# Two PSUM pools instead of one, feed-forward work in smaller parts, and the key and query products moved from GpSimd to VectorE

## The chip, the cores and the metric

The kernel runs on one core of a Trainium2 chip. The core has a matrix engine (TensorE, PE in the profile, with its weight loads as PEld), a vector engine (VectorE, DVE), an activation engine (ScalarE, ACT), a general engine (GpSimd, POOL) and a queue for transfers (SyncE, SP). Matrix products land in PSUM, which this kernel uses as eight banks of 512 fp32 numbers for each of 128 partitions. The metric is device time in microseconds for the whole program; the inputs lie in device memory before it and the output lies there after it.

## The reference, cut to what matters

Two blocks follow each other. The first is a recurrent attention with a complex gate, for 4 batches, 8 heads, 768 positions and 48 features a head; the second is a feed-forward block with a maximum over three products.

```python
def _attn_ref(q, k, v, a_re, a_im):
    mag = np.sqrt(a_re * a_re + a_im * a_im)
    scale = np.minimum(mag, 0.999) / (mag + 1e-06)
    a_re_n, a_im_n = (a_re * scale, a_im * scale)
    for t in range(S):                      # S = 768
        new_re = ar * S_re - ai * S_im      # S_re, S_im: (B, H, D, D)
        new_im = ar * S_im + ai * S_re
        S_re, S_im = (new_re + k[t] v[t], new_im)
        y[t] = q[t] S_re

def _moe_ref(x, w1, w2, w3, w_out):         # x: 3072 x 384, w1..w3: 384 x 768
    h = np.maximum(np.maximum(x @ w1, x @ w2), x @ w3)
    return h @ w_out                        # 3072 x 384
```

The kernel does not step through positions one by one. It takes 128 positions of one batch as a tile (24 tiles, two to a group, so 12 groups), turns the gate into a logarithm of its size (`Ln`) and an angle, sums these within the tile by matrix products, scales the keys and queries by the exponentials of the sums, and gets the scores, the carried state and the output from matrix products. Everything is fp32.

## The kernel before: the parts that the change touches

Every PSUM tile comes from one pool with one tag: four rooms of two banks each, which go round in the order in which the tiles are asked for.

```python
    psum = ctx.enter_context(tc.tile_pool(name="psum", bufs=4, space=PSUM))
    # ...
    def banks(nm, n=None):
        ps = psum.tile([P, 2, 512], FP, tag="ps", name=nm)
        return ps if n is None else ps.rearrange("p a n -> p (a n)")[:, 0:n]
```

From group 2 on, the matrix engine's order is fixed as written (`chained`): each matrix product is tied behind the last. The orders of the other engines come from the scheduler when the program is built.

The products of keys and queries with their decays stand behind the sums. `E` has two buffers.

```python
    def products(x):
        g, c = divmod(x, C)
        def s0():
            ps = banks("sums")
            # ... 8 matrix products
            En = T["En", x] = nat2.tile([P, DM], FP, tag="En", name="En")
            act(out=En.rearrange("p (c n) -> p c n", c=2), in_=ps[:, :, HC:2 * HC], func=AF.Exp, scale=-1.0)
            for nm, sg in (("k", 1.0), ("q", -1.0)):
                E = nat2.tile([P, DM], FP, tag="E", name="E")
                act(out=E.rearrange("p (c n) -> p c n", c=2), in_=ps[:, :, 0:HC], func=AF.Exp, scale=sg)
                eng = nc.gpsimd if g > 1 else nc.vector
                eng.tensor_tensor(out=hd(T[nm, x]), in0=E, in1=hd(T[nm, x]), op=OP.mult)
        # ...
```

The scores come in two tiles. `A` is put into the score matrix `atm` by four masked copies on VectorE; after them ScalarE copies `B` into the same `atm`.

```python
    def scores(x, nm):
        ps = banks(nm)
        # ... "A": 32 matrix products of 80 columns, "B": 16 of 32 columns
    def gather(x, nm):
        atm = T["atm", x] = atms[x % 2]
        if nm == "A":
            # ... nc.vector.copy_predicated, four times, from T["A", x]
        else:
            src = T[nm, x][:, 0, 0:H * 32].rearrange("p (h t) -> p h t", h=H)
            for o in (0, L64):
                nc.scalar.copy(out=atm[o:o + 32, :, 32:], in_=src[o:o + 32])
```

The feed-forward block: a step takes three column blocks of 128 (`n = 3`), so its PSUM tile is 768 numbers wide for the two tiles of a group. The first of three weights is copied to `hT` by ScalarE, the second and third are joined by a maximum on VectorE.

```python
    def up_step(xs, fs, i):
        # ...
        ps = banks("up", len(fs) * n).rearrange("p (f t) -> p f t", t=n)
        for j, f in enumerate(fs):
            for d in range(KD):
                mm(out=ps[:, j], lhsT=ws[i][:, d, f * P:(f + 1) * P], rhs=xT[:, d],
                                 start=(d == 0), stop=(d == KD - 1))
        if i == 0:
            nc.scalar.copy(out=dst, in_=ps)
        else:
            nc.vector.tensor_tensor(out=dst, in0=dst, in1=ps, op=OP.max)

    def out_step(xs, x):
        ps = banks("op", DM)
        for f in range(KF):
            mm(out=ps, lhsT=hT[:, f, o:o + P], rhs=wo[:, f], start=(f == 0), stop=(f == KF - 1))
        ot = fp2.tile([P, DM], FP, tag="ot", name="ot")
        nc.scalar.copy(out=ot, in_=ps)
        # ... store

    def ffn_steps(xs):
        n = 2 if xs[0] == 0 else 3
        return [call(up_step, xs, range(f, f + n), i) for f in range(0, KF, n) for i in range(3)] \
            + [call(out_step, xs, x) for x in xs]
```

One group mixes attention for its tiles x and y with the feed-forward steps of the group before and the gates of the groups after. `feed(n)` issues the next n feed-forward steps; `pairs` is both scores with their gathers; `turned` holds the transposes (`tp`, evicted to `K` and `Q`), the cut sums (`F`, evicted to `f` by four ScalarE exponentials), and the state (`dk`, added to `g` by VectorE); `sums` are the two `s0` above; `turning` holds the angles (`cs`); `later` are the gates of the group after next.

```python
        if g > 1:
            feed(1)
        pairs(x)
        if g > 1:
            gates[2]()
        feed(1)
        # ...
        turned(y)
        sums[0]()
        sums[1]()
        feed(1)
        outputs(x, tokens(x))
        rest(y)
        turning()          # feeds 2 steps before its matrix products
        pairs(y)
        units[0]()
        units[1]()
        for f in later:
            f()
        feed(2)
        turned(y + 1)
        feed(1)
        outputs(y, tokens(y))
        rest(y + 1)
        feed(len(ffn))
```

Of the kernel before, what the change touches and what calls it, by code (L numbers as in the profile page):

```python
# [51 lines left out]
def kernel(  # L52
# [22 lines left out]
    C = 2  # L75
# [484 lines left out]
    def scores(x, nm):  # L560

        ps = banks(nm)
        for h in range(H):
            if nm == "A":
                for o in range(0, P, 32):
                    mm(out=ps[o:o + 32, h // HU, h % HU * P:h % HU * P + 80], lhsT=T["K", x][0:DD, h, o:o + 32],
                       rhs=T["Q", x][0:DD, 4 * h + o // 32], start=True, stop=True)
            else:
                for j in range(2):
                    o = j * L64  # L570
                    mm(out=ps[o:o + 32, 0, h * 32:h * 32 + 32], lhsT=T["KB", x][0:DD, 2 * h + j],
                       rhs=T["QB", x][0:DD, 2 * h + j], start=True, stop=True)
        T[nm, x] = ps

    def gather(x, nm):
# [24 lines left out]
        else:  # L600
            src = T[nm, x][:, 0, 0:H * 32].rearrange("p (h t) -> p h t", h=H)
            for o in (0, L64):
# [58 lines left out]
    def up_step(xs, fs, i):  # L661
        xT, n = T["xT", xs[-1]], len(xs) * P
        if fs[0] == 0 and i == 0:

            T["hT", xs[-1]] = ld2.tile([P, KF, n], FP, tag="ar", name="hT") if xs[0] == 0 else \
                fp2.tile([P, KF, n], FP, tag="hT", padded_shape=[P, KF, TG], name="hT")
        dst = T["hT", xs[-1]][:, fs[0]:fs[-1] + 1]
        ps = banks("up", len(fs) * n).rearrange("p (f t) -> p f t", t=n)
        for j, f in enumerate(fs):
            for d in range(KD):  # L670
                mm(out=ps[:, j], lhsT=ws[i][:, d, f * P:(f + 1) * P], rhs=xT[:, d],
                                 start=(d == 0), stop=(d == KD - 1))
        if i == 0:
            nc.scalar.copy(out=dst, in_=ps)  # L674
        else:
            nc.vector.tensor_tensor(out=dst, in0=dst, in1=ps, op=OP.max)  # L676

    def out_step(xs, x):
        hT, o = T["hT", xs[-1]], (x - xs[0]) * P
        ps = banks("op", DM)  # L680
        for f in range(KF):
            mm(out=ps, lhsT=hT[:, f, o:o + P], rhs=wo[:, f], start=(f == 0), stop=(f == KF - 1))
        ot = fp2.tile([P, DM], FP, tag="ot", name="ot")
        nc.scalar.copy(out=ot, in_=ps)
        t0 = x // C // NS * C * S + x % C * S + x // C % NS * P
        nc.sync.dma_start(out=out[t0:t0 + P, :], in_=ot)

# [85 lines left out]
    weave((0.0, 1.0, tile_steps(0) + tile_steps(1)), (0.0, 0.7, rounds), (0.15, 0.58, pre_steps(1)),  # L773
          (0.415, 0.44, ffn[:6]), (0.55, 0.75, ffn[6:9]), (0.25, 0.27, [call(load, 1, load_v)]), (0.6, 0.62, [call(load, 2, load_a)]),
          (0.75, 1.0, gate_steps(2, list(range(C)))))
# [4 lines left out]

    held = ffn[9:]

    def group(g):
        x, y = g * C, g * C + 1
        load(g + 1, load_v)
        if g > 1:
            load(g + 2, load_a, load_kq)
        ffn = held + ffn_steps(tokens(x - 1))
        held[:] = [ffn.pop()]

        def feed(n):
            for _ in range(min(n, len(ffn))):
                ffn.pop(0)()
# [36 lines left out]
        sums[1]()  # L830
        feed(1)
        outputs(x, tokens(x))
# [14 lines left out]
    for g in range(1, NG):  # L847
        if g == 2:
            T["chain"] = None
        group(g)  # L850
    for f in held + ffn_steps(tokens(NX - 1)):
        f()
# [30 lines left out]
```

## Time and profile before

| what | value |
|---|---|
| time, median of 3 runs | 667.38 us (666.75 to 668.34) |
| span of the profiled execution | 666.7 us |
| PE busy | 581.8 us (87%), 10076 instructions |
| PEld busy | 472.5 us (71%) |
| DVE busy | 476.9 us (72%), 638 instructions |
| ACT busy | 404.2 us (61%), 670 instructions |
| POOL busy | 122.4 us (18%), 131 instructions |
| chain that ended last, by engine | PE 46%, ACT 24%, DVE 16% |
| granted PE clock, mean | 0.963 |

The busy time of an engine is the union of its instructions' times. "Idle before, releaser" in the profile is the time an engine stood still before an instruction, and what ended it. The chain that ended last is followed back from the last instruction, at each step to what released it. The first 150 us or so are a ramp, in which the weights are loaded and brought into shape; after it the kernel repeats one pattern for each group, and that pattern is what the windows of the trace show best.

### The profile page before, as it was taken

Reading aid. Unit: us, or ns where it says so; the run is one execution under the profiler, and the core shown is the slowest. Engines: PE = TensorE matmul, PEld = TensorE weight load, DVE = VectorE, ACT = ScalarE, POOL = GpSimd, SP = SyncE. Lnnn points to the kernel's source line nnn. Section 1 sums busy time; section 2 is a strip of 40 time slices with the busy share of each in tenths; the row PEclk is TensorE's granted clock in tenths of the full one; section 3 lists DMA queues with packets and bytes.
Section 4 is the critical chain, followed back from the end, with each engine's and each line's share of the span. In section 5 each row is a group of like instructions: output and inputs, shape, how many; then the busy total and the mean of one; then the engine's idle time right before and its main releaser. Section 6 shows DMA issues by size and latency. Waiting matters only on the chain.

```text
span 666.7 us, 22815 instructions
## 1 busy us (share of the span) xinstructions
PE 581.8 (87%) x10076; PEld 472.5 (71%) x10076; DVE 476.9 (72%) x638; ACT 404.2 (61%) x670; POOL 122.4 (18%) x131
## 2 busy tenths in 40 slices
PE   1244777898999999999999999999999999999997
PEld 0143665777877878868868867878878777878785
DVE  3899998985777877877776687778778777655111
ACT  6889696577476567567566665765764854631000
POOL 9400102305113114013014013023023023000000
PEclk9956898997999999999999999999999999999999
DMA  6975542330330330330330420421320210000000
GB/s 134 272 166 142 139 83 56 62 62 14 61 65 24 61 69 19 65 69 15 73 61 15 83 52 24 76 53 35 67 56 15 40 47 3 2 27 2 19 7 24
DMA packets 136547, 39.26 MB, mean 59 GB/s; under 512 B 129152, under 2 KB 132224, under 8 KB 136448
## 3 DMA queue, kind: packets, MB, share of 16 engines
q1 hardware_dynamic: 136448, 37.80, 26.1%
q8 instruction: 79, 1.29, 0.8%
q14 instruction: 20, 0.16, 0.1%
HBM read 33.03 MB, written 4.72 MB: 57 GB/s over the span
## 4 chain that ended last, share of the span: by engine, by line
PE 46%; ACT 24%; DVE 16%; issue 8%; DMA 3%; SPq 2%; POOL 1%; DVEq 0%; POOLq 0%; ACTq 0%
PE up L117 24%; PE op L117 12%; DVE Q L533 6%; PE y L117 3%; ACT CS L112 3%; ACT f L112 2%; ACT L133 2%; ACT e L112 2%; PE A L117 2%; ACT Q L505 2%; PE cs L117 2%; ACT K L501 2%; PE dk L117 2%; DVE g L632 2%; DMA ai<-in_a_im_dram 1%
## 5 line engine op out<-in xcount | busy, mean ns | idle before, releaser
L117 PE MATMUL up<-xT,w 128*128 128x256 f32 (+1 forms) x1404 | 295.9, 369 | 11.0 <-ACT f L112 4.5
L117 PEld LDWEIGHTS up<-xT,w 128*128 128x128 f32 x1404 | 249.0, 192 | 46.9 <-ACT f L112 7.7
L533 DVE TENSOR_TENSOR Q<-Q,f 112x512 f32<-112x512 f32 (+2 forms) x72 | 91.6, 1278 | 49.2 <-ACT f L112 49.2
L117 PE MATMUL op<-wo,hT 128*128 128x384 f32 x288 | 99.0, 494 | 0.5 <-ACT K L501 0.4
L117 PEld LDWEIGHTS op<-wo,hT 128*128 128x128 f32 x288 | 53.2, 190 | 34.9 <-DVE hT L676 0.8
L674 ACT COPY hT<-up 128x768 f32<-128x768 f32 (+2 forms) x27 | 19.6, 727 | 91.8 <-PE up L117 91.7
L676 DVE TENSOR_TENSOR hT<-hT,up 128x768 f32<-128x768 f32 (+2 forms) x54 | 46.4, 859 | 38.8 <-PE up L117 38.7
L381 POOL TENSOR_TENSOR ai<-ai,L 128x768 f32<-128x768 f32 x10 | 22.3, 2226 | 276.9 <-ACT L L112 188.0
L117 PE MATMUL A<-Q,K 112*32 112x80 f32 x1536 | 34.7, 247 | 12.8 <-DVE Q L533 12.8
L117 PEld LDWEIGHTS A<-Q,K 112*32 112x32 f32 x1536 | 29.9, 117 | 21.8 <-issue 13.6
L117 PE MATMUL y<-atm,vb 128*32 128x64 f32 x1152 | 39.5, 224 | 0.9 <-issue 0.7
L117 PEld LDWEIGHTS y<-atm,vb 128*32 128x32 f32 x1152 | 32.6, 112 | 10.4 <-issue 5.6
L112 ACT ACTIVATE f<-F 48x280 f32<-48x280 f32 x96 | 38.3, 399 | 0.9
L117 PE MATMUL y<-QG,g 112*32 112x64 f32 x1408 | 38.3, 220 | 0.0
L487 DVE TENSOR_TENSOR uk<-uk,En 128x768 f32<-128x768 f32 x24 | 24.5, 1021 | 18.0 <-PE tp L117 18.0
L477 POOL TENSOR_TENSOR k<-E,k 128x384 f32<-128x384 f32 x20 | 25.6, 1279 | 63.7 <-ACT E L112 63.7
L389 POOL TENSOR_TENSOR ai<-ai,carry 1x768 f32<-1x768 f32 x10 | 18.6, 1864 | 92.8 <-ACT ai L386 92.8
L117 PE MATMUL sums<-Ln,mid 64*64 64x192 f32 x192 | 15.8, 378 | 22.7 <-DVE Ln L371 22.7
L117 PEld LDWEIGHTS y<-QG,g 112*32 112x32 f32 x1408 | 34.9, 110 | 0.4 <-ACT g L630 0.2
L477 POOL TENSOR_TENSOR q<-E,q 128x384 f32<-128x384 f32 x20 | 34.9, 1747 | 0.0
L117 PE MATMUL cs<-w,upto 128*64 128x192 f32 x192 | 20.1, 355 | 15.7 <-DVE w L400 15.7
L412 DVE SCALAR_TENSOR_TENSOR nf<-t,cs 128x384 f32<-128x384 f32 x24 | 13.3, 554 | 28.5 <-ACT t L410 27.4
(103 smaller groups left out, 949.9 us busy)
## 6 DMA issues: line engine op xcount, KB each, us to landing
ar<-in_a_re_dram SPq DMA_DIRECT2D x24, 192.0 KB
ai<-in_a_im_dram SPq DMA_DIRECT2D x24, 192.0 KB
k<-in_k_dram SPq DMA_DIRECT2D x96, 48.0 KB
q<-in_q_dram SPq DMA_DIRECT2D x96, 48.0 KB
vb<-in_v_dram SPq DMA_DIRECT2D x96, 48.0 KB
out_dram<-ot SPq DMA_DIRECT2D x24, 192.0 KB
raw<-in_moe_w_dram SPq DMA_DIRECT2D x5, 768.0 KB
w<-in_moe_w_dram SPq DMA_DIRECT2D x2, 768.0 KB
```

The source lines that it names most:

```text
L112: tab(nc.scalar.activation(**kw))
L117: ins = f(**kw)
L133: tab(nc.scalar.preload_act_table_set(nm))
L381: (nc.gpsimd if g > 1 else nc.vector).tensor_tensor(out=ai, in0=ai, in1=L, op=OP.mult)
L389: nc.gpsimd.tensor_tensor(out=ai[0:1], in0=ai[0:1], in1=T["carry", g], op=OP.subtract)
L477: eng.tensor_tensor(out=hd(T[nm, x]), in0=E, in1=hd(T[nm, x]), op=OP.mult)
L487: nc.vector.tensor_tensor(out=u, in0=u, in1=two(T["En", x]), op=OP.mult)
L501: nc.scalar.copy(out=T["K", x][0:DD].rearrange("p n (j t) -> p j n t", j=2), in_=src)
L505: nc.scalar.copy(out=T["Q", x][0:DD, :, 0:32].rearrange("p (n j a) t -> p j n a t", n=H, j=2), in_=src.rearrange("p j n (a t) -> p j n a t ...
L533: nc.vector.tensor_tensor(out=out, in0=in_, in1=f.to_broadcast([DD, 2 * H - g, n, 8]), op=OP.mult)
L674: nc.scalar.copy(out=dst, in_=ps)
L676: nc.vector.tensor_tensor(out=dst, in0=dst, in1=ps, op=OP.max)
```

## The change

The PSUM pool is split in two: `psum2` with three rooms of two banks, for the tiles that need two (`A`, `tp`, `F`, `dk`, `sums`), and `psum1` with two rooms of one bank, for the others (`B`, `cs`, `y`, `up`, `op`). The eight banks are as before all in use, as five rooms and not four. So that a feed-forward tile fits one bank, a step takes two column blocks in place of three, in all tiles. The steps are cut into parts (half an `up` step, a third of an `op` step) which `feed` counts, and `feed` is called at one more place, between the transposes and the state, so that the matrix engine has work there. Last, the products of keys and queries are made by VectorE for all groups; before, GpSimd made them for the groups 2 to 11. What is computed stays the same.

```diff
-    psum = ctx.enter_context(tc.tile_pool(name="psum", bufs=4, space=PSUM))
+    psum1 = ctx.enter_context(tc.tile_pool(name="psum1", bufs=2, space=PSUM))
+    psum2 = ctx.enter_context(tc.tile_pool(name="psum2", bufs=3, space=PSUM))
@@ banks
-        ps = psum.tile([P, 2, 512], FP, tag="ps", name=nm)
-        return ps if n is None else ps.rearrange("p a n -> p (a n)")[:, 0:n]
+        if n is None:
+            return psum2.tile([P, 2, 512], FP, tag="two", name=nm)
+        return psum1.tile([P, 512], FP, tag="one", name=nm)[:, 0:n]
@@ products
-                eng = nc.gpsimd if g > 1 else nc.vector
+                eng = nc.vector
@@ scores
-        ps = banks(nm)
+        ps = banks(nm, None if nm == "A" else H * 32)
@@ up_step, now a list of parts (out_step alike, three parts of two blocks each)
+        def part(j, f):
+            # ...
+            if j == 0:
+                box["ps"] = banks("up", len(fs) * n).rearrange("p (f t) -> p f t", t=n)
             for d in range(KD):
-                mm(out=ps[:, j], lhsT=ws[i][:, d, f * P:(f + 1) * P], rhs=xT[:, d],
+                mm(out=box["ps"][:, j], lhsT=ws[i][:, d, f * P:(f + 1) * P], rhs=xT[:, d],
+            # ... the eviction after the last part
+        return [call(part, j, f) for j, f in enumerate(fs)]
@@ ffn_steps
-        n = 2 if xs[0] == 0 else 3
-        return [call(up_step, xs, range(f, f + n), i) for f in range(0, KF, n) for i in range(3)] \
-            + [call(out_step, xs, x) for x in xs]
+        return [up_step(xs, (f, f + 1), i) for f in range(0, KF, 2) for i in range(3)] \
+            + [out_step(xs, x) for x in xs]
@@ group
-        ffn = held + ffn_steps(tokens(x - 1))
-        held[:] = [ffn.pop()]
+        ffn = held + every_part(ffn_steps(tokens(x - 1)))
+        held[:] = ffn[-3:]
+        del ffn[-3:]
-        pre = pre_steps(g + 1, feed) if g + 1 < NG else [lambda: None] * 8
+        pre = pre_steps(g + 1, lambda n: feed(2 * n)) if g + 1 < NG else [lambda: None] * 8
@@ turned
                 cut(x)
+            feed(2)
             state(x - 1)
@@ the body of the group
         if g > 1:
-            feed(1)
+            feed(3)
         pairs(x)
         ...
-        feed(1)
+        feed(2)
         ...
         sums[1]()
-        feed(1)
+        feed(2)
         outputs(x, tokens(x))
         ...
-        feed(2)
+        feed(6)
         turned(y + 1)
-        feed(1)
+        feed(3)
         outputs(y, tokens(y))
```

More of the change, by code (lines that the diff above doesn't have):

```diff
@@ L570, in scores @@
                     o = j * L64
-                    mm(out=ps[o:o + 32, 0, h * 32:h * 32 + 32], lhsT=T["KB", x][0:DD, 2 * h + j],
+                    mm(out=ps[o:o + 32, h * 32:h * 32 + 32], lhsT=T["KB", x][0:DD, 2 * h + j],
                        rhs=T["QB", x][0:DD, 2 * h + j], start=True, stop=True)
@@ L600, in gather @@
         else:
-            src = T[nm, x][:, 0, 0:H * 32].rearrange("p (h t) -> p h t", h=H)
+            src = T[nm, x].rearrange("p (h t) -> p h t", h=H)
             for o in (0, L64):
@@ L661, in up_step @@
     def up_step(xs, fs, i):
[L662 to L669, printed above, removed]
-            for d in range(KD):
-                mm(out=ps[:, j], lhsT=ws[i][:, d, f * P:(f + 1) * P], rhs=xT[:, d],
-                                 start=(d == 0), stop=(d == KD - 1))
@@ L673, in up_step @@
[L673 to L676, printed above, removed]
-    def out_step(xs, x):
[L679 to L686, printed above, removed]
+        n, box = len(xs) * P, {}
@@ new lines, in part @@
+        def part(j, f):
+            xT = T["xT", xs[-1]]
+            if f == 0 and i == 0:
+                T["hT", xs[-1]] = ld2.tile([P, KF, n], FP, tag="ar", name="hT") if xs[0] == 0 else \
+                    fp2.tile([P, KF, n], FP, tag="hT", padded_shape=[P, KF, TG], name="hT")
+            if j == 0:
+                box["ps"] = banks("up", len(fs) * n).rearrange("p (f t) -> p f t", t=n)
+            for d in range(KD):
+                mm(out=box["ps"][:, j], lhsT=ws[i][:, d, f * P:(f + 1) * P], rhs=xT[:, d],
+                   start=(d == 0), stop=(d == KD - 1))
+            if j < len(fs) - 1:
+                return
+            dst = T["hT", xs[-1]][:, fs[0]:fs[-1] + 1]
+            if i == 0:
+                nc.scalar.copy(out=dst, in_=box["ps"])
+            else:
+                nc.vector.tensor_tensor(out=dst, in0=dst, in1=box["ps"], op=OP.max)
@@ new lines, in up_step, with part @@
+        return [call(part, j, f) for j, f in enumerate(fs)]
+    def out_step(xs, x):
+        box = {}
+        def part(j):
+            hT, o = T["hT", xs[-1]], (x - xs[0]) * P
+            if j == 0:
+                box["ps"] = banks("op", DM)
+            for f in (2 * j, 2 * j + 1):
+                mm(out=box["ps"], lhsT=hT[:, f, o:o + P], rhs=wo[:, f], start=(f == 0), stop=(f == KF - 1))
+            if j < KF // 2 - 1:
+                return
+            ot = fp2.tile([P, DM], FP, tag="ot", name="ot")
+            nc.scalar.copy(out=ot, in_=box["ps"])
+            t0 = x // C // NS * C * S + x % C * S + x // C % NS * P
+            nc.sync.dma_start(out=out[t0:t0 + P, :], in_=ot)
+        return [call(part, j) for j in range(KF // 2)]
@@ L703, in ffn_steps, with every_part @@
     def ffn_steps(xs):
-        n = 2 if xs[0] == 0 else 3
-        return [call(up_step, xs, range(f, f + n), i) for f in range(0, KF, n) for i in range(3)] \
-            + [call(out_step, xs, x) for x in xs]
+        return [up_step(xs, (f, f + 1), i) for f in range(0, KF, 2) for i in range(3)] \
+            + [out_step(xs, x) for x in xs]
+    def every_part(steps):
+        return [part for step in steps for part in step]
     def front(x):
@@ L773 @@
     weave((0.0, 1.0, tile_steps(0) + tile_steps(1)), (0.0, 0.7, rounds), (0.15, 0.58, pre_steps(1)),
-          (0.415, 0.44, ffn[:6]), (0.55, 0.75, ffn[6:9]), (0.25, 0.27, [call(load, 1, load_v)]), (0.6, 0.62, [call(load, 2, load_a)]),
+          (0.415, 0.44, every_part(ffn[:6])), (0.55, 0.75, every_part(ffn[6:9])), (0.25, 0.27, [call(load, 1, load_v)]), (0.6, 0.62, [call(load, 2, load_a)]),
           (0.75, 1.0, gate_steps(2, list(range(C)))))
     load(2, load_kq)
-    held = ffn[9:]
+    held = every_part(ffn[9:])
     def group(g):
@@ L850 @@
         group(g)
-    for f in held + ffn_steps(tokens(NX - 1)):
+    for f in held + every_part(ffn_steps(tokens(NX - 1))):
         f()
```

## The prediction

> **What bounds it now.** I read the busy times by window first, to see what limits the repeating part; then the waits in that part; then the order of instructions in one group. The windows' columns are: busy time and count of PE, PEld, DVE, ACT and POOL, the granted PE clock, and the DMA share.
>
> ```profile
> 50.00:100.00 50.00, 30.61 (x642) 26.88 (x638) 47.43 (x72) 42.70 (x69) 1.81 (x1) 0.81 0.52 121
> 250.00:300.00 50.00, 48.27 (x883) 38.70 (x885) 38.54 (x49) 31.82 (x53) 9.89 (x6) 1.00 0.26 51
> ```
>
> In the ramp VectorE is full (47.43 of 50) and TensorE waits. From about 200 us on TensorE is busy for 48.27 of 50 us at full clock and VectorE has a quarter of its time free. A group lasts 48.95 us there: its first `A` starts at 250.62, the next group's at 299.56. So TensorE bounds eight or nine of the twelve groups, and each microsecond that it stands still is lost. What stops it, in one group:
>
> ```profile
> 260.67 4.15 PE L117 MATMUL up<-xT,w 128*128 128x256 f32 x18 [0.44 <-ACT f L112]
> 267.15 8.04 PE L117 MATMUL up<-xT,w 128*128 128x256 f32 x36 [0.60 <-DVE g L633]
> 288.56 1.14 PE L117 MATMUL dk<-vb,uk 64*64 64x48 f32 x64 [0.68 <-DVE hT L676]
> ```
>
> Each of the three waits for a PSUM room, of `F`, `dk` and `up`. They make 0.44 + 0.60 + 0.68 = 1.72 us a group, so the group's own matrix work is 48.95 - 1.72 = 47.2 us. That is all that better rooms can win: 1.7 us in each of some nine groups, 15 us.
>
> **The Trainium skill.** Three places bear on it. "GPSIMD Engine Reference", 3.1 Elementwise, puts a two-input elementwise operation on GpSimd at 1.96 times VectorE's time. The trace has a larger ratio: 1.32 (k) and 1.72 us (q) median on GpSimd, 0.57 us for the same 128x384 shape on VectorE in the first groups. Section 1, Specifications, says GpSimd shares its SBUF interfaces with VectorE, with contention when VectorE has two SBUF inputs. The trace agrees: the state's first product, a 112x384 with two SBUF inputs, takes 1.35 us at 263.60, while GpSimd makes q, and 0.55 us at 293.45, while it does nothing. "TensorE: Matmul & The Clock Gate" says two things: in "Architectural detail", that ScalarE and VectorE are strictly first in, first out; in Part 1, that the clock halves after an idle window of some 3.4 us. The trace agrees with the second after a stop of 4.70 us:
>
> ```profile
> 102.36 2.36 PE L117 MATMUL A<-Q,K 112*32 112x80 f32 x64 [4.70 <-DVE Q L533]
> 276.57 1.31 PE L117 MATMUL A<-Q,K 112*32 112x80 f32 x64
> ```
>
> The same 64 instructions took 2.36 us after the stop and 1.31 us without.
>
> **Part by part: the products.** Forty of them, four for each of ten groups, leave GpSimd: 20 x 1.279 + 20 x 1.747 = 60.5 us off an engine that nobody in the repeating part waits for long. On VectorE they cost 40 x 0.57 = 22.8 us, 2.3 us a group. VectorE gets about as much back, since the products that ran beside GpSimd (Q 1.95 for 1.22, g 1.35 for 0.55) shrink by some 2 us. In busy time this part is nearly neutral; in order it is not, as the four stand in VectorE's queue ahead of `hT`.
>
> **Part by part: smaller steps.** Evictions of `up` go from 27 to 39 on ScalarE and 54 to 78 on VectorE, with the same elements in all. A 128x768 takes 0.95 us on VectorE and a 128x256 0.41, so about 0.14 us fixed each: 24 x 0.14 = 3.4 us on VectorE, 12 x 0.16 = 2 us on ScalarE. Beside TensorE this hides.
>
> **Part by part: the rooms.** Here the path changes. The order in which the changed program is built fixes who waits for whom. The one-bank tiles now have two rooms, so each waits until the tile two places earlier is evicted; before, it was four places. I walk through a group with the durations above. An `up` step is now 6 products, which the trace records as 12 instructions; 36 of them took 7.97 us, so a step is 12 x 0.221 = 2.66 us. A takes 1.2 us, B 0.6, the two transposes and F 1.7, dk 1.1, sums 1.85, y 1.7, cs 1.45, an `op` step 4.07.
>
> First half, A at 0: the `up` steps, transposes, dk and sums find their rooms free, because the masked copies end at about 3.4 and B's copy at 4.1. The third `up` ends at 14.25 and y at 15.95. The next `up` needs the room of the third, whose maximum is behind this line on VectorE, from F's exponentials at 8.6: Q (0.61), Q (1.14), hT (0.55), Q (0.87), g, KB, g, QB, g (0.46 or 0.60 each), four products (0.45 to 0.57, the third and fourth held by E's two buffers), hT. That is done at about 17.2. TensorE waits 1.2 us. cs then starts at about 22.6.
>
> Second half, cs at 0: A, B and one `up` follow and end at 5.85. The second `up` takes the room of B. Before, B's room was wanted only after two steps of 4 us and a transpose. ScalarE frees it with its copy into `atm`, and this copy now stands in ScalarE's order behind the angles' functions, a table load, and three of the gates' functions (L, w, e). The kernel before shows how long those take:
>
> ```profile
> 276.03 0.49 ACT L410 ACTIVATE t<-cs 128x384 f32<-128x384 f32 x1
> ...
> 280.58 1.28 ACT L133 ACT_TABLE_LOAD   x1
> 281.88 0.84 ACT L112 ACTIVATE L<-L 128x768 f32<-128x768 f32 x1
> 282.63 0.72 ACT L603 COPY atm<-B 32x256 f32<-32x256 f32 x2
> 283.37 0.84 ACT L112 ACTIVATE w<-L 128x768 f32<-128x768 f32 x1
> 284.12 0.83 ACT L112 ACTIVATE e<-L 128x768 f32<-128x768 f32 x1
> ```
>
> From the first t (0.85 after cs starts) to the end of the table load is 281.86 - 276.03 = 5.83, so 6.7; L, w and e add 0.75 + 0.75 + 0.85, B's copy 0.72: done at 9.75. TensorE waits 9.75 - 5.85 = 3.9 us, in each group from 2 to 9. In group 10, without gates after it, the copy follows the table load and the wait is 1.5.
>
> A third stop: the second `op` needs the room of the first, whose copy on ScalarE stands behind the next gate's square, which waits for w on VectorE, behind the whole chain Q to g. By the same sums that square is done at about 28.4 after cs, the copy at 28.9, and TensorE wants the room at 26.8 (all with the 3.9 us stop). 1 to 2 us more; I take 1.6.
>
> **The sum.** Stops of 1.2 + 3.9 + 1.6 = 6.7 us in place of 1.72: +5.0 us a group. A stop of 3.9 us may halve the clock; a window of 3.4 us falls mostly into it about half the time, and costs some 1.7 us then: +0.9. Eight groups: 8 x 5.9 = 47. Group 10 about +1, the tail 0 (only `up` and `op` steps, VectorE free). In the ramp VectorE is full, and takes up 4 x 0.57 for group 2 and the more evictions: +3. Together +51, so 718 us.
>
> **Rivals.** First, the rooms do what they are for: the three waits of 1.72 us go, VectorE and GpSimd no longer meet, and the time falls by up to 15 us to 652. For it: all three waits are for rooms, and there are five rooms now. Against it: the two rooms of the short tiles are wanted sooner than they are freed, by the order as built; one B in each group is enough. Second, VectorE becomes the bound by its load: 477 + 23 + 3 - 20 = 483 us of some 670 says no; in a group it has 38.5 of 49 us. It would give 670 to 680. Third, the stops are there, but shorter, since the engines run ahead of my walk: only the 3.9 us one, and at full clock: 8 x (3.9 - 1.7) = 18, so 685. Against it: all three stops follow from ScalarE's and VectorE's own orders.
>
> **Range and chances.** The stop behind B is the surest: it is one chain of ScalarE with known durations. The other two hang on long sums and may be 0 to 2.5 us each; the clock may give nothing or twice what I took. Low end: 8 x (3.9 + 0.7 - 1.7) + 5 = 28, so 696. High end: 8 x (4.5 + 2 + 2.3 - 1.7 + 1.2) + 6 = 72, so 739. Faster by 2% (under 654) needs the first rival to hold entirely: 0.03. Within 2% (to 681): 0.06. Slower: 0.91.
>
> **What would show it.** In a window of the repeating part PE busy falls from 48.3 to about 43 or 44 of 50. The waits of that part have a new first row for PE: `up` waiting for the ScalarE copy into `atm`, some 3.9 us each, eight times; then `up` waiting for hT and `op` for ot. The group's period is 54 to 55 us. The clock in these windows falls below 1.00. GpSimd's busy time falls to about 62 us, VectorE's rises to some 483, and no 112x384 state product of VectorE takes 1.35 us in the first half. I am wrong if the period is under 50, if `up` finds B's room free, or if the loss lies in the ramp and not in the groups.

## The result, and the profile after

The changed kernel takes **757.94 us** (median of 4 runs, 757.29 to 759.13). The kernel before took 667.07 us on the same chip (4 runs, 665.96 to 668.34). The ratio is 1.136, with a 95% interval of 1.134 to 1.139. So the change costs 91 us, where the prediction had 51 us and a range that ended at 739 us.

The page of the kernel after, its busy times (us, share of the span, instructions):

```profile
PE 622.3 (82%) x10076; PEld 489.6 (65%) x10076; DVE 472.5 (62%) x702; ACT 408.1 (54%) x682; POOL 60.7 (8%) x91
```

Two things are to be seen in it. TensorE has the same 10076 matrix instructions as before but is busy for 622.3 us and not 581.8: 40.5 us more, so the same instructions took longer. And the span minus its busy time went from 666.7 - 581.8 = 84.9 us to 757.4 - 622.3 = 135.1 us: it stands still for 50.2 us more. The two make the 90.7 us of the span. VectorE and GpSimd have less to do, or the same: 472.5 (476.9 before) and 60.7 us (122.4 before).

The waits of TensorE in the repeating part (from 180 to 640 us) of the kernel after; the columns are the time in total, how often, and the longest:

```profile
PE up L118 <- ACT atm L605: 31.9, 8, 4.0
PE op L118 <- ACT ot L701: 15.2, 7, 2.3
PE up L118 <- DVE hT L684: 11.7, 7, 1.8
```

These are the three stops that the prediction walked out, at the tiles it named. The largest is the second `up` step of a group's second half, which waits for the room that ScalarE's copy of `B` into `atm` frees. The time line of TensorE from 301.19 us on (the second half of group 4 and the first half of group 5) shows them one after the other (start, duration, operation, count; in brackets the idle time before and who ended it):

```profile
309.77 6.98 PE L118 MATMUL up<-xT,w 128*128 128x256 f32 x24 [3.98 <-ACT atm L605]
...
322.07 4.14 PE L118 MATMUL op<-wo,hT 128*128 128x384 f32 x12
330.23 5.69 PE L118 MATMUL op<-wo,hT 128*128 128x384 f32 x12 [2.29 <-ACT ot L701]
...
352.51 5.45 PE L118 MATMUL up<-xT,w 128*128 128x256 f32 x24 [1.31 <-DVE hT L684]
```

In it, the same 24 instructions of `up` take 6.98 us behind the stop of 3.98 us and 5.45 us behind the one of 1.31 us. The same 12 of `op` take 5.69 us behind the stop of 2.29 us and 4.14 us without one. Windows of one microsecond around the two longer stops say why. Their columns are the busy time and count of PE, PEld, DVE, ACT and POOL, the granted clock, the DMA share and its GB/s:

```profile
308.00:309.00 1.00, 0.00 (x0) 0.00 (x0) 1.00 (x3) 1.00 (x2) 0.00 (x0) 1.00 0.40 72
309.00:310.00 1.00, 0.23 (x1) 0.23 (x2) 0.61 (x2) 0.96 (x4) 0.00 (x0) 0.75 0.45 78
...
312.00:313.00 1.00, 1.00 (x4) 0.75 (x3) 0.40 (x1) 0.56 (x1) 0.00 (x0) 0.54 0.37 66
313.00:314.00 1.00, 1.00 (x7) 0.87 (x5) 0.69 (x1) 0.28 (x1) 0.00 (x0) 1.00 0.42 78
...
330.00:331.00 1.00, 0.77 (x1) 0.50 (x2) 1.00 (x2) 0.97 (x3) 0.00 (x0) 0.50 0.00 0
333.00:334.00 1.00, 1.00 (x4) 0.66 (x3) 0.00 (x0) 0.00 (x0) 0.00 (x0) 0.80 0.35 65
```

The clock is 1.00 while TensorE stands still, and falls to 0.50 just as it goes on, for about 3.4 us each time (309.5 to 313, and 330 to 333.4). Half a clock for 3.4 us of work loses 1.7 us; here TensorE goes on some 0.3 us after the clock has fallen, and `up` loses 6.98 - 5.45 = 1.53 us, `op` 5.69 - 4.14 = 1.55 us. So a stop that halves the clock costs its own length and some 1.5 to 1.7 us more.

ScalarE's own order at that time, in which the copy that frees the room stands last:

```profile
305.35 1.28 ACT L135 ACT_TABLE_LOAD   x1
306.64 0.84 ACT L113 ACTIVATE L<-L 128x768 f32<-128x768 f32 x1
307.52 0.84 ACT L113 ACTIVATE w<-L 128x768 f32<-128x768 f32 x1
308.27 0.83 ACT L113 ACTIVATE e<-L 128x768 f32<-128x768 f32 x1
309.00 0.72 ACT L605 COPY atm<-B 32x256 f32<-32x256 f32 x2
```

The copy takes 0.72 us for both halves together; what makes it late are the table load and the gates' functions ahead of it, 3.65 us from 305.35 to 309.00.

Where the 91 us lie along the kernel is read from the starts of `A` in the even tiles, the length of each group in us:

| group | 0 | 1 | 2 | 3 | 4 | 5 | 6 | 7 | 8 | 9 | 10 |
|---|---|---|---|---|---|---|---|---|---|---|---|
| before | 57.2 | 45.6 | 53.6 | 48.9 | 48.9 | 48.2 | 47.3 | 49.1 | 48.9 | 48.9 | 48.0 |
| after | 56.7 | 54.1 | 59.8 | 61.0 | 59.4 | 57.2 | 58.2 | 60.8 | 57.7 | 55.5 | 53.7 |

From start to start the groups 2 to 9 lose 469.65 - 394.09 = 75.6 us, group 1 loses 8.5 and group 10 loses 5.7. All the rest together, the ramp before group 1 and the tail, is 1 us. The eight groups in one window each, before and after, with the columns of the windows above:

```profile
147.97:542.06 394.09, 379.17 (x6690) 306.02 (x6689) 297.65 (x370) 255.44 (x420) 80.30 (x48) 0.99 0.24 49
155.75:625.40 469.65, 408.60 (x6690) 317.71 (x6689) 292.75 (x417) 257.86 (x428) 28.23 (x16) 0.94 0.20 41
```

TensorE stands still for 469.65 - 408.60 = 61.0 us in place of 14.9: 46 us are stops. Of its busy time 51.0 us lie at the halved clock (6.3 before), and half of that is lost: 22 us are clock. What is left, its work at full clock, is 383 us in place of 376, although the count of instructions is the same: 7 us, or 0.9 us a group, that neither stops nor clock explain.

### The profile page after: what moved, and what is told of

Its sections match the earlier page's. It is cut to its first block, busy times and chain, and to the rows that moved or that the text cites. A ratio compares the mean times of both kernels' runs of the same rounds, so it can differ in the third digit from the quotient of the medians.

```text
span 757.4 us, 22669 instructions
## 1 busy us (share of the span) xinstructions
PE 622.3 (82%) x10076; PEld 489.6 (65%) x10076; DVE 472.5 (62%) x702; ACT 408.1 (54%) x682; POOL 60.7 (8%) x91
## 4 chain that ended last, share of the span: by engine, by line
issue 47%; PE 27%; DVE 12%; ACT 11%; DMA 1%; SPq 1%; POOL 0%; DVEq 0%; POOLq 0%; ACTq 0%
PE up L118 16%; PE op L118 6%; DVE Q L535 3%; ACT f L113 2%; DVE hT L684 1%; PE A L118 1%; ACT L L113 1%; ACT Q L507 1%; DMA w<-in_moe_w_dram 1%; PE y L118 1%; ACT CS L113 1%; ACT L135 1%; ACT K L503 1%; PE tp L118 1%; DVE k L479 1%
## 5 line engine op out<-in xcount | busy, mean ns | idle before, releaser
L118 PE MATMUL up<-xT,w 128*128 128x256 f32 (+1 forms) x1404 | 326.1, 388 | 54.5 <-ACT atm L605 34.5
L118 PEld LDWEIGHTS up<-xT,w 128*128 128x128 f32 x1404 | 261.7, 202 | 100.9 <-ACT atm L605 38.5
L118 PE MATMUL op<-wo,hT 128*128 128x384 f32 x288 | 109.3, 534 | 15.2 <-ACT ot L701 15.2
L535 DVE TENSOR_TENSOR Q<-Q,f 112x512 f32<-112x512 f32 (+2 forms) x72 | 75.4, 1072 | 50.3 <-ACT f L113 50.2
L684 DVE TENSOR_TENSOR hT<-hT,up 128x512 f32<-128x512 f32 (+1 forms) x78 | 50.1, 642 | 86.8 <-PE up L118 86.7
L682 ACT COPY hT<-up 128x512 f32<-128x512 f32 (+1 forms) x39 | 21.6, 553 | 60.3 <-PE up L118 60.2
L581 DVE COPY_PREDICATED atm<-maskd,A 128x512 f32<-128x512 uint8 x24 | 17.5, 730 | 50.0 <-PE A L118 50.0
L701 ACT COPY ot<-op 128x384 f32<-128x384 f32 x24 | 11.5, 477 | 56.7 <-PE op L118 56.5
L361 ACT ACTIVATE L<-ai 128x768 f32<-128x768 f32 (+1 forms) x13 | 10.3, 792 | 47.6 <-DVE w L384 36.4
L113 ACT ACTIVATE E<-sums 128x384 f32<-128x384 f32 x48 | 22.0, 491 | 25.8 <-DVE k L479 25.7
L503 ACT COPY K<-tp 112x1024 f32<-112x1024 f32 x24 | 24.3, 1012 | 21.5 <-PE tp L118 21.4
L605 ACT COPY atm<-B 32x256 f32<-32x256 f32 x48 | 17.2, 358 | 33.7 <-DVE atm L581 33.4
```

What stands on the lines that cost most here:

```text
L113: tab(nc.scalar.activation(**kw))
L118: ins = f(**kw)
L361: nc.scalar.activation(out=L, in_=ai, func=AF.Square)
L503: nc.scalar.copy(out=T["K", x][0:DD].rearrange("p n (j t) -> p j n t", j=2), in_=src)
L535: nc.vector.tensor_tensor(out=out, in0=in_, in1=f.to_broadcast([DD, 2 * H - g, n, 8]), op=OP.mult)
L581: nc.vector.copy_predicated(out=out, mask=mask, data=data)
```

## The experiments

Each ratio is against the kernel before on the same chip, with its 95% interval. The twelve together:

| run | what it is | us | ratio |
|---|---|---|---|
| changed kernel | | 757.94 | 1.136 [1.134, 1.139] |
| e1_b_two | `B` in a room of two banks | 717.95 | 1.077 [1.074, 1.080] |
| e2_gpsimd | products back on GpSimd | 773.66 | 1.161 [1.158, 1.163] |
| e4_fill | unused products fill the two longer stops | 733.12 | 1.100 [1.097, 1.102] |
| e5_ot_first | the copy into `ot` ahead of the square | 735.51 | 1.103 [1.101, 1.105] |
| e6_b_two_ot | e1 and e5 together | 689.46 | 1.033 [1.031, 1.036] |
| e8_all | e6, and the third stop repaired | 657.12 | 0.985 [0.982, 0.987] |
| e10_all_gpsimd | e8 with the products on GpSimd | 691.11 | 1.036 [1.034, 1.038] |
| e11_all_b_one | e8 with `B` in a room of one bank | 683.76 | 1.024 [1.021, 1.027] |
| e12_no_max | e8 with the products in their old place | 674.17 | 1.009 [1.007, 1.011] |
| e3_before_vector | the kernel before, products on VectorE | 662.51 | 0.993 [0.991, 0.996] |
| e7_before_small | the kernel before, steps of two blocks | 685.57 | 1.029 [1.027, 1.032] |
| e13_old_max | e3, products behind the maximum | 659.10 | 0.987 [0.985, 0.989] |

The theory after the result: the loss is made by three waits for rooms, and by the clock, which the two longer ones halve. The rivals: the products on VectorE do it; the smaller steps do it; or the stops alone do it and the clock is a bystander.

### Is it B's room?

`B` goes into the pool of three two-bank rooms, and nothing else changes:

```diff
-        ps = banks(nm, None if nm == "A" else H * 32)
+        ps = banks(nm)
```

> The changed kernel, with B alone moved to the pool of two-bank rooms. Theory A (one-bank rooms are wanted before they are free, and each stop over some 2 us also halves the clock for one 3.4 us stretch): the stop of 3.98 us behind B's copy and the 1.7 us of half clock after it go, and about 1 us comes back where the third step now waits for the first one's maximum; 8 groups x 4.7 = 38 us less than 758: 720 us, 708 to 730. Theory B (the products on VectorE delay everything): unchanged, over 750. Theory C (the smaller steps cost TensorE and the evicting engines more): unchanged, over 750.

Measured: 717.95 us (717.2 to 719.65), 40 us less for one tile. The wait for `atm` is gone from the repeating part. The first `A` of group 2 starts at 148.03 us (155.75 in the changed kernel, 147.97 before), so the loss ahead of it hangs on `B`'s room too. It is not the same stop, though: in group 1 of the changed kernel `up` waits for `atm` 0.53 us only, and how the room costs time there stays open. TensorE's waits in the repeating part of this run:

```profile
PE up L118 <- DVE hT L684: 23.8, 16, 1.8
PE op L118 <- ACT ot L701: 20.3, 7, 3.2
```

The other two stops are left, one is there twice in a group, and the one behind `ot` grew from 2.3 to as much as 3.2 us, so a part of the gain is given back there.

### Is it the copy into ot?

ScalarE may start the next gate's second square only after the copy of the first `op`:

```diff
-            nc.scalar.activation(out=L, in_=ai, func=AF.Square)
+            sq = nc.scalar.activation(out=L, in_=ai, func=AF.Square)
+            if "ot" in T:
+                tc.add_manual_dep(sq.ins, T["ot"].ins.name, order, reason="ot first")
...
-            nc.scalar.copy(out=ot, in_=box["ps"])
+            T["ot"] = nc.scalar.copy(out=ot, in_=box["ps"])
```

In the changed kernel the square stood ahead of the copy and itself waited for VectorE, as ScalarE's time line shows there:

```profile
328.83 0.84 ACT L361 ACTIVATE L<-ai 128x768 f32<-128x768 f32 x1 [6.26 <-DVE w L384]
329.70 0.48 ACT L701 COPY ot<-op 128x384 f32<-128x384 f32 x1
```

> The changed kernel, with ScalarE's next gate square placed behind the copy of the op tile instead of ahead of it; rooms and everything else as changed. Theory A with the cost of the clock: the stop of 2.2 us ahead of the second op goes in 7 to 8 groups, and the 1.7 us of half clock behind it: 758 - 7.5 x 3.9 = 729, 719 to 739. Without the cost of the clock: 758 - 7.5 x 2.2 = 741 or more.

Measured: 735.51 us (734.72 to 735.8). No `op` waits for `ot` any more. The gain of 22.4 us over seven such stops is 3.2 us each, more than the 2.2 us that one of them lasts on average (15.2 / 7): about a microsecond of each is clock, which was halved behind five of the seven.

With both repairs at once, `B`'s room and the copy's place:

```diff
-        ps = banks(nm, None if nm == "A" else H * 32)
+        ps = banks(nm)
...
+            if "ot" in T:
+                tc.add_manual_dep(sq.ins, T["ot"].ins.name, order, reason="ot first")
```

> Both of these: B in the two-bank pool, and the op copy ahead of the square. In the kernel with B alone moved the stops ahead of the second op were 2.9 us each. Theory A: 718 - 8 x (2.9 + 1.7) = 681, 671 to 692; the stops of 1.3 us behind the two maxima stay. Theory C: well over 700, as the steps stay small.

Measured: 689.46 us (687.63 to 690.1). What is left are two short stops in a group, at a clock of 1.00 all the way from 250 to 550 us:

```profile
322.31 5.45 PE L118 MATMUL up<-xT,w 128*128 128x256 f32 x24 [1.31 <-DVE hT L686]
337.89 2.86 PE L118 MATMUL up<-xT,w 128*128 128x256 f32 x12 [1.29 <-DVE hT L686]
```

The two repairs bring 68.5 us together, and 40.0 + 22.4 = 62.4 apart.

### Is it the stop alone, or the clock behind it?

In the groups 1 to 9, eight matrix products whose result nobody uses are put where `up` waits for `B`'s room, and four where the second `op` waits. The rooms come free when they did before; TensorE is only kept at work meanwhile:

```diff
+    def fill(g, n):
+        ps = banks("fill").rearrange("p a n -> p (a n)")
+        for _ in range(n):
+            mm(out=ps[:, 0:TG], lhsT=ws[0][:, 0, 0:P], rhs=ws[1][:, 0, 0:TG], start=True, stop=True)
...
-        feed(6)
+        feed(2)
+        if later:
+            fill(g, 8)
+        feed(4)
         turned(y + 1)
...
         outputs(y, tokens(y))
+        if later:
+            fill(g, 4)
```

> The changed kernel with 12 matrix products a group more, in groups 2 to 9, of constant weights into a two-bank room that nothing reads: 8 in the stop behind B, 4 in the stop behind the first op. Theory A, clock included: TensorE stays busy, the clock stays at 1.00 there, and 2 x 1.7 us a group come back: 8 x 3.4 = 27 less, 731 us, 722 to 740, although more is computed. Without a cost of the clock (the longer matrix time has another cause): 758 or more.

Measured: 733.12 us (732.14 to 733.64): a kernel that does more matrix work is 24.8 us faster than the changed one. Its time line of TensorE:

```profile
296.16 3.62 PE L118 MATMUL fill<-w,w 128*128 128x256 f32 x16
300.31 5.45 PE L118 MATMUL up<-xT,w 128*128 128x256 f32 x24 [0.53 <-ACT atm L605]
...
319.23 4.14 PE L118 MATMUL op<-wo,hT 128*128 128x384 f32 x12 [0.37 <-ACT ot L701]
```

The fill takes 3.62 us, `up` still waits for `atm` at its end, and the `up` behind it takes 5.45 us and not 6.98. The clock is 1.00 from 250 to 550 us. The expectation speaks of the groups 2 to 9; the trace has 24 instructions of the fill in each of nine groups, 1 to 9. Of the gain, 22 us lie in the groups 2 to 9 (447.4 in place of 469.6 us), 2.8 us a group: that is what the halved clock costs there, apart from the stops themselves. The rival in which it is a bystander falls.

### Is it the products on VectorE?

The changed kernel with the products of the groups 2 to 11 back on GpSimd:

```diff
-                eng = nc.vector
+                eng = nc.gpsimd if g > 1 else nc.vector
```

> The changed kernel, with the products of keys and queries of groups 2 to 11 back on GpSimd, and nothing else. Theory A: only the stop of 1.3 us behind hT can go, and VectorE's slowed operations come back: 742 to 758 us. Theory B: most of the loss goes, below 690. Theory C: over 745.

Measured: 773.66 us (773.31 to 775.48), above the range of theory A and far above that of theory B (theory C's "over 745" holds it, but says nothing of these products): the products on VectorE do not cost anything, they save 16 us. TensorE and VectorE in this run, the stop that was 1.31 us long, and what comes before it:

```profile
357.17 7.13 PE L118 MATMUL up<-xT,w 128*128 128x256 f32 x24 [2.43 <-DVE hT L684]
```

```profile
352.34 1.48 DVE L535 TENSOR_TENSOR KB<-K,f 112x512 f32<-112x512 f32 x1
...
355.17 1.35 DVE L634 TENSOR_TENSOR g<-g,f 112x384 f32<-112x384 f32 x1
```

While GpSimd makes a product, VectorE's own products of two SBUF inputs take more than twice as long (`KB` 1.48 us here, 0.68 us when it is alone). They stand ahead of `hT`, so the maximum, and the room it frees, come later than if VectorE had made the four products itself. And with 2.43 us this stop halves the clock too: the 24 instructions behind it take 7.13 us, not 5.45. Most of the 16 us is clock: the seven stops behind `hT` from 180 to 640 us grow from 11.7 to 15.3 us in all, 3.6 us, and behind each of the seven `up` takes 7.13 us in place of 5.45, 11.8 us.

The same edit in the kernel before, the other way round (products on VectorE):

```diff
-                eng = nc.gpsimd if g > 1 else nc.vector
+                eng = nc.vector
```

> The kernel before, with the products of all groups on VectorE, and nothing else. Theory A: the four rooms hide it, within 1% of 667. Theory B: over 700. Theory C: within 1% of 667.

Measured: 662.51 us (661.16 to 663.29), 4.5 us less than before. This one line of the change, alone, makes the kernel faster, by 0.7%. The wait of `up` for `g` is gone; those of `dk` for `hT` (0.69 us) and of `up` for `f` (0.45 to 0.63 us) are left, and a group lasts 48.3 us.

### Is it the smaller steps?

The kernel before, with its four rooms and the products on GpSimd, with steps of two column blocks and one more step fed at three places:

```diff
-        n = 2 if xs[0] == 0 else 3
+        n = 2
...
-        pre = pre_steps(g + 1, feed) if g + 1 < NG else [lambda: None] * 8
+        pre = pre_steps(g + 1, lambda n: feed(n + 1)) if g + 1 < NG else [lambda: None] * 8
...
-        feed(1)
+        feed(2)
         if g == 1:
...
-        feed(2)
+        feed(3)
         turned(y + 1)
```

> The kernel before, with its four rooms of two banks and its products on GpSimd, but with steps of two column blocks (and one feed more at three places, so that the groups hold nearly the same matrix work at the same places). Theory A: small steps alone do no harm beyond a short stop or two, 662 to 690. Theory C (the smaller steps are the cause): over 710.

Measured: 685.57 us (685.28 to 688.01). TensorE's busy time is that of before in all (582.1 us against 581.8); in the repeating part a group's 852 matrix instructions keep it busy for 47.6 us in place of 47.2. So the smaller steps cost some 0.3 us a group in themselves. Most of the 19 us is waits:

```profile
PE up L117 <- DVE g L633: 12.6, 7, 1.9
```

A likely reason is that a shorter step leaves less time until its room is wanted again; this was not tested apart from the added feeds. `up` behind `g` waited 0.60 us in the kernel before and waits 1.9 us here.

### What is left when all three stops are repaired?

To e6 come two edits for the two stops behind `hT`. The four products go behind the maximum in VectorE's order, with `E` in four buffers and not two. And two parts of the feed-forward work are issued ahead of the angles' matrix products:

```diff
-                E = nat2.tile([P, DM], FP, tag="E", name="E")
+                E = fp4.tile([P, DM], FP, tag="E", name="E")
...
-                eng = nc.vector
-                eng.tensor_tensor(out=hd(T[nm, x]), in0=E, in1=hd(T[nm, x]), op=OP.mult)
+                def mult(E=E, nm=nm):
+                    ins = nc.vector.tensor_tensor(out=hd(T[nm, x]), in0=E, in1=hd(T[nm, x]), op=OP.mult)
+                    if g > 2:
+                        tc.add_manual_dep(ins.ins, T["max"].ins.name, order, reason="the maximum first")
...
         pairs(y)
+        feed(2)
         units[0]()
         units[1]()
         for f in later:
             f()
-        feed(6)
+        feed(4)
         turned(y + 1)
```

> Both of the first two, and two changes of order on VectorE: the four products stand behind the maximum of the step ahead of y (E has four buffers for that), and one feed-forward step is issued ahead of the angle products of the second half, so that its maximum is not behind all of them. Theory A: the last two stops of 1.3 us go too, which leaves the matrix work of 47.2 us a group: 660, 650 to 672. If the room count had no merit at all, it would stay near 681.

Measured: **657.12 us** (654.51 to 657.59), 1.5% under the kernel before (interval 1.3 to 1.8%) and 13% under the changed one. A window of its repeating part, with the columns of the windows above, is full:

```profile
250.00:300.00 50.00, 49.87 (x907) 39.65 (x908) 38.02 (x55) 32.32 (x55) 2.32 (x1) 1.00 0.25 50
```

TensorE is busy for 49.87 of 50 us, and the groups 2 to 10 last 46.9 to 48.4 us. Nothing of the matrix work was taken away; less than its busy time is not to be had from waits alone. That busy time has grown: a group of 852 matrix instructions takes 47.8 us here, where the kernel before takes 47.2 us for as many (48.94 less 1.73 of stops). A part of this is seen in e7_before_small (47.6); why smaller pieces in another order take longer was not taken further.

To see which of the two edits did which, the products go back to their old place, and the rest stays:

```diff
@@ against e8_all
-                def mult(E=E, nm=nm):
...
+                nc.vector.tensor_tensor(out=hd(T[nm, x]), in0=E, in1=hd(T[nm, x]), op=OP.mult)
...
-        for f in T.pop("mults", []):
-            f()
```

> The repaired version of five rooms (657.12 us) with the products back where they were, ahead of the third step's maximum in VectorE's order; the four E buffers and the feed-forward step ahead of the angle products stay. Theory (VectorE's place for the products sets the stop behind hT in the first half): the stop of 1.31 us is back in the groups 3 to 10, so 8 x 1.31 = 10 us, 667 us (662 to 674), with TensorE waiting for hT once a group at 1.0 to 1.8 us. Rival (E's two buffers held the products and with them the maximum; with four it is in time anyhow): 657 us within 3, and no wait for hT.

Measured: 674.17 us (673.16 to 674.25), 0.2 us above the theory's range and far from the rival's 657. The one stop is back, and VectorE's time line in front of it holds the four products between `QB` and the maximum, where the prediction had placed them. The stop of the second half stays away, so it was the feed ahead of the angles that removed that one:

```profile
310.48 0.69 DVE L537 TENSOR_TENSOR QB<-Q,f 112x512 f32<-112x512 f32 x1
311.08 0.55 DVE L481 TENSOR_TENSOR k<-E,k 128x384 f32<-128x384 f32 x1
311.55 0.55 DVE L481 TENSOR_TENSOR q<-E,q 128x384 f32<-128x384 f32 x1
312.02 0.55 DVE L481 TENSOR_TENSOR k<-E,k 128x384 f32<-128x384 f32 x1
312.49 0.55 DVE L481 TENSOR_TENSOR q<-E,q 128x384 f32<-128x384 f32 x1
312.96 0.55 DVE L636 TENSOR_TENSOR g<-g,f 112x384 f32<-112x384 f32 x1
313.43 0.68 DVE L686 TENSOR_TENSOR hT<-hT,up 128x512 f32<-128x512 f32 x1
```

The stops make 13.3 us in the groups 3 to 10; the run is 17 us slower than e8_all. The other 3.7 us are in group 2 (51.8 us against 48.1), which has the same stop, long enough there to halve the clock (7.11 us for 5.45):

```profile
164.01 7.11 PE L119 MATMUL up<-xT,w 128*128 128x256 f32 x24 [2.26 <-DVE hT L686]
```

In this repaired order, the products on GpSimd (in their old place, `E` still in four buffers):

```diff
@@ against e8_all, instead of mult
+                eng = nc.gpsimd if g > 1 else nc.vector
+                eng.tensor_tensor(out=hd(T[nm, x]), in0=E, in1=hd(T[nm, x]), op=OP.mult)
```

> The kernel with all four repairs, with the products of groups 2 to 11 on GpSimd. Theory A: rooms in order leave little for the products to spoil, but VectorE is slowed beside GpSimd as before (Q 1.95 for 1.22, g 1.35 for 0.55), so the maximum ahead of y comes later and stops of up to 1 us may return: 659 to 672. If the engine of the products made the difference by itself, as in the changed kernel (774 against 758), 16 us: 673.

Measured: 691.11 us (690.31 to 692.11), above both expectations. It is 34 us above e8_all, and 17 us above e12_no_max, which differs from it in the engine alone. So the same line is worth 4.5 us in the old rooms, 16 us in the changed kernel and 17 us in the repaired one at the same place. To move the products behind the maximum, on VectorE, is worth another 17 us (e8_all against e12_no_max); whether GpSimd's products would gain from such an order was not tested. VectorE and GpSimd show the same picture as in e2_gpsimd:

```profile
318.09 1.50 DVE L538 TENSOR_TENSOR QB<-Q,f 112x512 f32<-112x512 f32 x1
319.51 1.34 DVE L637 TENSOR_TENSOR g<-g,f 112x384 f32<-112x384 f32 x1
```

```profile
319.00 1.44 POOL L482 TENSOR_TENSOR q<-E,q 128x384 f32<-128x384 f32 x1
```

```profile
321.51 7.04 PE L119 MATMUL up<-xT,w 128*128 128x256 f32 x24 [2.43 <-DVE hT L687]
```

`QB` and `g` take 1.50 and 1.34 us beside GpSimd, 0.69 and 0.55 us in the run above, and the maximum behind them comes later by as much.

And the repaired order with `B` in a one-bank room again:

```diff
@@ against e8_all
-        ps = banks(nm)
+        ps = banks(nm, None if nm == "A" else H * 32)
```

> The kernel with all four repairs, with B alone put back into the one-bank rooms, as in the changed kernel. Theory A: one stop of about 4 us in the groups 1 to 9, with a half clock of 1.7 us behind most: 657 + 9 x 5 = 702, 690 to 712. If the stop behind B mattered only beside the others: below 675.

Measured: 683.76 us (682.4 to 685.14), between the two expectations and in neither: `B`'s room still costs 27 us, but the stop that was expected did not come. What TensorE waits for in this run:

```profile
334.16 5.45 PE L119 MATMUL up<-xT,w 128*128 128x256 f32 x24 [1.81 <-DVE hT L695]
```

In the groups 2 to 9 no `up` waits for `atm`. The copy of `B` is as late as ever and ends at 336.29 us, but the second `up` step starts at 334.16, right behind the first step's maximum: it was given the room of the first step and not `B`'s. So the two rooms are not simply taken in turns; what decides was not followed up. The clock stays whole behind these stops of 1.81 us (5.45 us for 24 instructions). Of the 28.3 us between the profiled spans of this run and e8_all (683.3 and 655.0), the eight groups with this stop make 14.7. Group 10, where `up` does wait 2.10 us for `atm` and the clock halves, makes 3.9, and 9.7 lie ahead of group 2, whose first `A` starts at 155.60 us (145.94 in e8_all), as late as in the changed kernel.

### Do the new rooms bring anything of their own?

The kernel before, its four rooms and its steps of three blocks, with the products on VectorE behind the maximum as in e8_all, and `E` in four buffers:

```diff
@@ against the kernel before
-                E = nat2.tile([P, DM], FP, tag="E", name="E")
+                E = fp4.tile([P, DM], FP, tag="E", name="E")
-                eng = nc.gpsimd if g > 1 else nc.vector
-                eng.tensor_tensor(out=hd(T[nm, x]), in0=E, in1=hd(T[nm, x]), op=OP.mult)
+                def mult(E=E, nm=nm): # as in e8_all
...
         feed(1)
+        for f in T.pop("mults", []):
+            f()
         outputs(x, tokens(x))
```

> The kernel before, its four rooms and steps of three blocks, with the products on VectorE behind the maximum of the step ahead of them, and E in four buffers. Theory (five rooms bring nothing of their own once all waits are repaired; the old rooms' last wait, dk for hT at 0.69 us, is one of VectorE's order): that wait goes, 8 x 0.69 = 5.5 us below the 662.51 us of the products on VectorE alone, 657 us (654 to 660). Rival (the five rooms and small steps are what won the rest): the wait stays or comes back at another tile, 662 us within 2.

Measured: 659.10 us (658.6 to 659.99). The time is in the theory's range and its reason is wrong: `dk` still waits for `hT` eight times, and the groups 3 to 10 are the length that they had in e3_before_vector (47.4 to 48.4 us). TensorE's waits in the repeating part:

```profile
PE dk L118 <- DVE hT L685: 5.5, 8, 0.7
```

That maximum belongs to the group's second half and has none of the products ahead of it. What it gains on e3_before_vector (3.4 us by the medians, 2.0 us between the two profiled spans, 658.3 and 660.3) lies at the beginning: the first `A` starts at 43.2 and not 44.8 us, the groups 0 and 1 are 1.8 us shorter together, and group 2 is 1.4 us longer. With the place and the buffers changed in one run, which of the two did it stays open. The answer to the question stands all the same: five rooms with everything repaired make 657.12 us, and four rooms with the products moved 659.10 us, with intervals that overlap. The cutting into parts and the additional feed between transposes and state are in all runs with five rooms; they were not tested apart.

## Why the prediction was right and wrong

**The walk through the rooms was right.** It gave three stops of 1.2, 3.9 and 1.6 us behind `hT`, `B`'s copy into `atm`, and `ot`; the stretch from 301 us on has 1.31, 3.98 and 2.29 us at those tiles. The one that it called the surest, the copy of `B` behind L, w and e, is right to 0.1 us. In that closeness is some luck, as both of its ends came 0.3 us later than walked: `up` ends 6.1 us after cs starts (5.85 said) and the copy 10.04 us (9.75 said). Its worth, 40 us, is shown by e1_b_two. The place of the four products ahead of the maximum is shown by e12_no_max. Only `ot` was sized too short, 1.6 for up to 2.29 us. In that stretch, stops of 7.58 us stand for 6.7. Two readings of the working are slightly off and move nothing: its own durations put the end of y at 16.13 and not 15.95 us, and the `A` read at 250.62 and 299.56 start at 250.55 and 299.49 us.

**The step that failed is the clock.** The prediction said of the 3.9 us stop that the clock may halve "about half the time" and put +0.9 us on a group for it, for that stop alone. The Trainium skill ("TensorE: Matmul & The Clock Gate", Part 1) has an idle window of some 3.4 us, and the prediction took it that a stop has to cover most of such a window. The trace agrees with the page in the length, 3.41 us, but not in the idleness. The clock halves behind all eight stops of 3.98 us in the groups 2 to 9, three times for two windows, and behind five of the six of 2.15 to 2.29 us, which leave a window partly busy: from 326.56 to 329.98 us, ahead of the halved clock at 330, TensorE works 1.37 us. A stop of 3.98 us, wherever it lies, covers at least 1.99 us of one window of 3.41, so "half the time" was too rare for it, and the stop behind `ot` had no clock in the sum at all. In the stretch from 301 us on, 7.58 us of stops, 1.53 + 1.55 = 3.1 us of clock and 47.7 us of work make the 58.4 us (301.2 to 359.6).

The sum of the eight groups, term by term: the clock costs 22 us, 2.8 us a group, where 0.9 was said. The stops cost 46 us, 5.8 a group where 5.0 was said. The work itself, taken as fixed at 47.2 us, is 0.9 us a group longer. So of the 28 us between the 75.6 measured and the 47 said, 15 are the clock, 6 the stops and 7 the work; the clock is the largest term, and e4_fill shows it by itself.

**Group 10 and the ramp.** Group 10 loses 5.7 us where +1 was said, group 1 8.5 us where the ramp with it was given +3. The prediction had VectorE's load in mind for the ramp, and that is not what cost there: with `B` in another room, the products still on VectorE, group 2 starts as early as in the kernel before. Group 10 has a stop behind `atm` of 2.10 us (1.5 said), and behind it the same 24 `up` instructions take 7.13 us.

**The products.** GpSimd's busy time was said to fall to some 62 us (60.7 measured). VectorE's was said to rise to 483 us and fell to 472.5, a likely reason being that more was slowed beside GpSimd than the 2 us a group that were reckoned; that was not taken apart. "In busy time nearly neutral; in order it is not" is half right: in order the products stand ahead of the maximum, but so do the products that GpSimd slows down, and these are worse. e2_gpsimd and e10_all_gpsimd missed by 16 us and more for the same reason. "GPSIMD Engine Reference", section 1 of the Trainium skill speaks of shared SBUF interfaces with contention; the trace agrees and gives the size, 0.68 to 1.48 us for a 112x512 product.

**A rule that was too strict.** The prediction let each one-bank tile wait for the tile two places earlier. That held in the changed kernel for `B` but not in e11_all_b_one, where the second step got the first step's room. The order as built has to be read for rooms too, tile by tile.

**The rivals.** The first, that the rooms do what they are for, is refuted for this kernel as built; e8_all shows that they could, and that they then win 10 us (all but 2 of which four rooms have too, in e13_old_max). VectorE as the bound is refuted by its 472.5 us of 757. The third, only the 3.9 us stop at full clock, would have been 685 us; all three stops are there, and the clock is not full.

## What to carry to other kernels

More, smaller rooms are not more room: count for each tile when its room is wanted again and where the eviction that frees it stands in the order of its engine, and keep a tile with a late eviction out of a pool of two. When TensorE is the bound, price a stop at its length, and one from about 1.9 us on at up to 1.7 us of halved clock besides, or twice that where it falls badly across two clock windows. Test it by putting unused products into it. If an engine that shares an input path with another takes over work, ask what stands beside it on the other and what waits behind that.

## What the runs showed of the hardware

- **The clock is set window by window, and the windows lie on a fixed grid.** In each of the fourteen traces, every change of the granted clock falls on a grid of 3.413 us, to within 1.2 ns; in the changed kernel, for example, at 309.50, 312.91, 329.98 and 333.39 us. How long TensorE was busy in one window goes with the clock of the next: behind windows at full clock after 150 us, the 60 halved windows follow a busy share of 0.46 or less, and the 2089 full ones a share of 0.42 or more. So it is not the length of a stop alone that counts but how much of it lies in one window. e10_all_gpsimd has the same stop of 2.21 us ahead of 424.26 us, where `up` takes 5.45 us, and ahead of 474.50, where it takes 7.13. The first reaches over into the next window, the second lies in one window alone. The windows that the two begin in, each with the one after it:

```profile
420.33:423.74 3.41, 1.72 (x112) 1.56 (x112) 3.41 (x5) 1.67 (x3) 2.87 (x3) 1.00 0.02 5
423.74:427.16 3.42, 2.90 (x13) 2.58 (x14) 3.32 (x4) 0.00 (x0) 0.00 (x0) 1.00 0.25 50
471.53:474.94 3.41, 1.20 (x57) 1.01 (x47) 3.41 (x5) 0.71 (x2) 1.90 (x2) 1.00 0.03 5
474.94:478.36 3.42, 3.42 (x10) 2.71 (x9) 2.47 (x3) 0.00 (x0) 0.00 (x0) 0.50 0.43 83
```

  In the same run a stop of 3.37 us, ahead of 169.36 us, left the clock whole, with shares of 0.49 and 0.53 in the two windows that it crosses; in e2_gpsimd one of 1.85 us, ahead of 415.27, halved it, with a share of 0.46.
- **A halved clock stays until a window is nearly full.** After 150 us, the ten halved windows with a busy share of 0.83 or less are each followed by another halved one, the 61 with 0.87 or more by a full one. So behind three of the eight stops of 3.98 us in the changed kernel the 24 instructions of `up` take 8.3 to 8.5 us and not 6.9 to 7.1, where 5.45 us is their time at full clock.
- **VectorE beside GpSimd.** In e2_gpsimd the product `QB` of two SBUF inputs (112x512) takes 1.49 to 1.50 us in all nine cases that lie wholly beside a product of GpSimd, 0.68 alone; `KB`, of the same shape, takes 1.02 to 1.49. `g` times `f` (112x384) takes 1.35 us in eight such cases and 0.55 alone. With one input in PSUM there is no difference: the maximum takes 0.68 us in eight such cases and alone, and the sum of `g` and `dk` 0.54 us in sixteen.
